# Half the tokens of six blocks through seven half-width products, with their activation sums on GpSimd

## The chip, the cores and the metric

The kernel runs on one core of one Trainium2 chip. The metric is the time of one execution on the device in microseconds; for the kernel before it is the median of three runs. The profile shows one execution, engine by engine: PE is TensorE, DVE VectorE, ACT ScalarE, POOL GpSimd and SP SyncE, which here only issues DMAs.

## The reference

An attention with a relative-position bias feeds a two-layer network with a snake-like activation (8 batches, 8 heads, 576 positions, head dimension 64; 512 wide, 2048 hidden):

```python
scores = scale * np.matmul(q, k.transpose(0, 1, 3, 2))
scores = scores + bias.transpose(2, 0, 1)[None, :, :, :]
attn = np.exp(scores - np.max(scores, axis=-1, keepdims=True))
attn = attn / (np.sum(attn, axis=-1, keepdims=True) + 1e-09)
x = np.matmul(attn, v).transpose(0, 2, 1, 3).reshape(4608, 512)
h = x @ w_in
s = np.sin(alpha * h)
g = h + s * s / (alpha + 1e-09)
out = g @ w_out
```

The 8 x 576 positions are the 4608 tokens (rows) of the second part.

## The kernel before

The tokens go through the second part in nine blocks of 512, numbered 0 to 8; the attentions go by batch, 0 to 7. The loop over `t` plans attention `t`, then the first layer and the activation of block `t` (`plan_moe_in`), then block `t`'s output matmuls (`plan_mo`), which run as filling during attention `t` + 1. Blocks 7 and 8 have no attention behind them; their output matmuls are the tail.

In an attention PE computes scores of two heads (`qT`, `kT`) into a pair of PSUM banks, ACT takes the exponential of a unit of 128x1024 into `u`, DVE multiplies the part near the diagonal by the exponential of the bias (`m2r`, `mhr`; lines 740 and 726: two SBUF inputs, written in place), and PE multiplies the result by `v`. DVE normalizes (lines 954 and 955) and SP's transposing DMAs, or PE, write the result into `xT`. Several units make a run: the first has three units of head pair 0 (key columns 0 to 2), the next a unit of the last 64 keys, the next the fourth column of pair 0 and two columns of pair 1. The product with `v` for pair 0 needs the bias multiplications of all four columns.

In the snake stage PE makes `h` for 16 slices of 128 hidden units, ACT takes the sine (line 1070), ACT or DVE squares it (lines 1077 and 1079), and DVE forms `g` (line 1084). A row is 128 tokens of a block; its output is 16 matmuls of 512 columns into one PSUM bank, which ACT or DVE copies to `outs` (lines 539 and 541) and SP stores.

The tail already uses Strassen's form in Winograd's variant (`plan_half`): for two rows together, the activations and `w_out` are split into 2 x 2 quarters, and seven products of 8 matmuls of 256 columns take the place of eight such products. It needs four sums of activation quarters (`pre`, 128x1024 elements) and four differences of weight quarters (`wsum`, made once by `plan_wsum` in attentions 2 to 5, one in each, in four pieces). The products are combined when they are taken from PSUM.

The order of every engine is fixed when the kernel is built. `Plan` holds tasks with dependencies, a priority and a planned duration for each engine that may do them, and picks the next by planned start and priority. Tasks with `fill` set are let into the attentions by a quota, or where PE would otherwise stand for longer than `FILL_GAP`. On the chip each engine keeps this order and waits on semaphores. PSUM banks are given out by tag (`BANKS`): `mo` and `av` share banks 6 and 7, scores and `h` use 0 to 5.

POOL issues the DMAs that convert types. When the first slice of `g` of block `b` is done, it loads `v` of batch `b` + 1 (`load_v16`) and stages `k` and `q` of batch `b` + 2 in DRAM as f16 (`stage_kq`). SP later transposes these into `kT` and `qT` (`load_kqT`), and POOL copies the last 64 keys of `kT` into `kt` (`load_kt`).

Of the kernel before, what the change touches and what calls it, by code (L numbers as in the profile page):

```python
# [10 lines left out]
F16 = mybir.dt.float16  # L11
# [29 lines left out]
class Task:  # L41
    def __init__(self, engs, emit, deps, pri, nb=0.0):
        self.engs, self.emit, self.deps, self.pri, self.nb = engs, emit, list(deps), pri, nb
        self.allocs = []
        self.marks = []
        self.offs = None
        self.s_only = self.fill = False
        self.pad = ()
        self.end = self.eng = None

# [11 lines left out]
class Plan:  # L62
# [86 lines left out]
    def run(self, t0):  # L149
        free = {e: t0 for e in ("PE", "ACT", "DVE", "POOL", "SP")}  # L150
        todo = list(self.tasks)
        while todo:
# [4 lines left out]
            for t in todo:  # L157
# [6 lines left out]
                for e in t.engs:  # L164
# [106 lines left out]
def kernel(  # L271
# [75 lines left out]

    xT = sgl.tile([128, NP, XN], F16, name="xT")
    wsum = sgl.tile([128, 4, NF // 2, DM // 2], F16, name="wsum")


    natx = tp.tile([128, NF * DM], F16, name="natx", tag="g", bufs=2)
# [24 lines left out]

    def new_sq():
        return tp.tile([128, DM], F16, name="sq", tag="sq", bufs=NBUF["sq"])

    def new_outs():
        return tp.tile([128, DM], F32, name="outs", tag="outs", bufs=NBUF["outs"])
# [3 lines left out]
    def bank(b, n=1):  # L386
        k = b.banks[0]
        return pb[:, k, :] if n == 1 else pb[:, k : k + n, :]

    def stage_kq(t):  # L390
        for dst, src in ((staged_k, k), (staged_q, q)):
            nc.gpsimd.dma_start(
                out=dst.ap()[t].rearrange("s (h d) -> s h d", h=H),
                in_=src[t].rearrange("h s d -> s h d"),
            )
# [138 lines left out]
    def k_of(e):  # L534
        return {"ACT": nc.scalar, "DVE": nc.vector, "POOL": nc.gpsimd}[e]
# [510 lines left out]
    def plan_moe_in(b, tbl):  # L1046
# [5 lines left out]
        for f in range(NF):  # L1052
# [28 lines left out]
            def gg(e, f=f, h=h, sq=sq):  # L1081
                if f == 0:
                    gcell[b].v = new_g()
                nc.vector.scalar_tensor_tensor(  # L1084
                    out=gcell[b].v[:, f, :], in0=sq.v, scalar=inv_a[:, f : f + 1], in1=h.v,
                    op0=ALU.mult, op1=ALU.add,
                )
# [10 lines left out]
            for n in steps:  # L1098
# [16 lines left out]
    mo_last = []  # L1115

    def plan_mo(b, a):

# [52 lines left out]
    def plan_half(b, a):  # L1171
# [21 lines left out]
        def pre(k, x, y, op, deps):  # L1193

            def sm(e):
                if k == 0:
                    u.v = new_u()
                nc.vector.tensor_tensor(out=sums(k), in0=x(), in1=y(), op=op)
# [69 lines left out]
        for (c0, c1), k in zip(cuts, "ef"):  # L1268
            p = prod(k, lambda: act(1, 1), ws(3), True, [], c0, c1)
            add(k, 2, (o2[0], 1, 0), [p, z], o2[1], False, c0, c1)  # L1270

    def set_table(name):
        nc.scalar.preload_act_table_set(name)  # L1273
        plan.sin = name == SIN_SET
# [8 lines left out]
    for t in range(T):  # L1283
# [29 lines left out]

        tbl = [plan.add({"ACT": D_TBL}, swap, exps, PB)]
        if 1 <= t < T - 1:
            plan.add({"SP": 5.5}, turn_in, [], PB + 9000, after=tbl + [
                x for tt, _, _, x in xdone if tt == t and "SP" in x.engs])
        if t == T - 1:
            tail_alone(t, PB + 10015)
        sins = []  # L1320
# [42 lines left out]
```

## Time and profile before

| what | value |
|---|---|
| median of 3 runs | 369.78 us (369.11 to 369.91) |
| the profiled execution | 369.14 us |
| its span, first to last instruction | 367.2 us |
| granted TensorE clock, mean over the span | 1.000 |
| time of one block in the middle (block 2's snake stage and attention 3) | 39.55 us |
| DMA, mean over the span | 110 GB/s |

How to read it: "busy" is the union of an engine's instructions. A row of the timeline gives the start (us from the span's start), the duration from the first to the last of a group, the engine, the source line, the operation, the tiles written and read, the shape and the count, and in brackets the idle time ahead of it with what ended it. Most matmuls are recorded on one helper line (459), so they are told apart by tiles: `xT,w_in` is the first layer, `w_out,g` the output, `wsum` a Strassen product, `qT,kT` the scores, `v,u` and `vh,u` the products with `v`. Matmuls overlap in time: the pace of a row of them is shorter than the duration of one.

### The profile page before, as it was taken

The page shows a single profiled execution, that of the slowest core. Times are in us where ns is not written, and L with a number is a line of the kernel's source. Part 1 is how long each engine was busy: PE and PEld are TensorE (multiplying, and loading weights), DVE is VectorE, ACT ScalarE, POOL GpSimd, SP SyncE. Part 2 cuts the span into 40 slices and gives each one's busy share as a digit, 9 for nine tenths or more (in the row PEclk, how much of TensorE's full clock was granted, in tenths as well). Part 3 has the DMA queues.
Part 4 walks back from the last instruction along what each step waited for, and adds up shares of the span by engine and source line. Part 5 has one row for each costly group of instructions (what it writes and reads, how often), then busy time and mean ns, then how long its engine had stood idle before and what let it go on. Part 6 is the DMA issues. An engine that isn't in the chain of part 4 may idle for free.

```text
span 367.2 us, 9181 instructions
## 1 busy us (share of the span) xinstructions
PE 359.4 (98%) x3664; PEld 204.4 (56%) x3664; DVE 279.2 (76%) x609; ACT 316.5 (86%) x437; POOL 91.7 (25%) x133
## 2 busy tenths in 40 slices
PE   7989999999999999999999999999999999999996
PEld 3564545644464455784554456445566455445885
DVE  4797957678777967697759777796769675999972
ACT  3998999899997999799989999799979997999411
POOL 8487350063000910064003700090006000000000
PEclk9999999999999999999999999999999999999999
DMA  9999999689624993199918992699339321000222
GB/s 169 204 160 203 198 165 155 145 71 131 120 59 96 107 167 91 51 160 143 131 48 145 125 166 61 109 98 181 77 68 159 71 59 49 8 1 31 71 75 86
DMA packets 150266, 40.49 MB, mean 110 GB/s; under 512 B 137208, under 2 KB 145616, under 8 KB 150224
## 3 DMA queue, kind: packets, MB, share of 16 engines
q0 software_dynamic: 96032, 17.67, 59.6%
q1 hardware_dynamic: 54016, 22.16, 25.2%
q8 instruction: 28, 0.46, 0.6%
q14 instruction: 14, 0.11, 0.1%
q10 hardware_dynamic: 176, 0.09, 0.1%
HBM read 37.73 MB, written 16.56 MB: 148 GB/s over the span
## 4 chain that ended last, share of the span: by engine, by line
PE 90%; ACT 6%; DVE 2%; issue 1%; ACTq 0%
PE pb L459 89%; ACT u L709 3%; ACT s L1070 1%; DVE u L740 1%; ACT sq L1077 1%; PE pb L1026 1%; PE pb L558 0%; ACT kT L539 0%; ACT qT L539 0%; PE pb L552 0%; DVE qT L541 0%; DVE xn L955 0%; DVE outs L1246 0%; DVE zz L510 0%; DVE u L726 0%
## 5 line engine op out<-in xcount | busy, mean ns | idle before, releaser
L709 ACT ACTIVATE u<-pb 128x1024 f16<-128x1024 f32 (+1 forms) x146 | 137.3, 1016 | 7.9 <-PE pb L459 6.4
L459 PE MATMUL pb<-xT,w_in 128*128 128x512 f16 (+4 forms) x704 | 127.6, 340 | 0.0
L459 PE MATMUL pb<-w_out,g 128*128 128x512 f16 (+1 forms) x512 | 119.0, 366 | 0.0
L1084 DVE SCALAR_TENSOR_TENSOR g<-sq,inv_a,pb 128x512 f16<-128x512 f16 x144 | 101.1, 742 | 4.5 <-ACT sq L1077 2.6
L1070 ACT ACTIVATE s<-pb,alphaT 128x512 f16<-128x512 f32 x144 | 93.0, 693 | 11.4 <-PE pb L459 10.4
L459 PEld LDWEIGHTS <-w_in 128*128 128x128 f16 x704 | 64.7, 98 | 57.2 <-issue 0.3
L740 DVE TENSOR_TENSOR u<-u,m2r 128x512 f16<-128x512 f16 (+1 forms) x128 | 62.0, 491 | 30.4 <-ACT u L709 27.9
L459 PEld LDWEIGHTS <-g 128*128 128x128 f16 x552 | 50.1, 98 | 47.4 <-issue 6.2
L459 PEld LDWEIGHTS <-u 128*128 128x128 f16 x1280 | 56.2, 97 | 11.3 <-issue 3.6
L404 POOL COPY kt<-kT 64x256 f16<-64x256 f16 x12 | 4.8, 396 | 171.4 <-DMA kT<-staged_k 171.2
L1077 ACT ACTIVATE sq<-s 128x512 f16<-128x512 f16 x73 | 45.5, 637 | 0.9
L459 PE MATMUL pb<-v,u 128*128 128x65 f16 x1024 | 44.0, 193 | 0.2 <-DVE u L740 0.2
L459 PE MATMUL pb<-qT,kT 64*128 64x64 f16 (+1 forms) x512 | 41.9, 285 | 1.7 <-ACT u L709 0.8
L1079 DVE TENSOR_TENSOR sq<-s 128x512 f16<-128x512 f16 x71 | 29.3, 421 | 12.5 <-ACT s L1070 11.5
L955 DVE TENSOR_TENSOR xn<-pb,rd 128x256 f16<-128x256 f32 (+2 forms) x59 | 28.5, 483 | 2.0
L459 PEld LDWEIGHTS <-kT 64*128 64x128 f16 x512 | 16.3, 94 | 22.9 <-issue 16.1
L459 PE MATMUL pb<-vh,u 128*128 128x130 f16 x128 | 28.2, 220 | 0.0
L409 POOL DMA_DIRECT2D v<-in_v_dram x28 | 24.8, 895 | 4.1 <-DMA nat<-in_k_dram 2.2
L954 DVE RECIPROCAL rd<-pb 128x4 f32<-128x4 f32 (+2 forms) x59 | 10.9, 185 | 13.2 <-PE pb L459 13.2
L541 DVE COPY outs<-pb 128x512 f32<-128x512 f32 x26 | 17.8, 685 | 3.0 <-PE pb L459 3.0
L1273 ACT ACT_TABLE_LOAD x15 | 19.2, 1283 | 0.3
L539 ACT ACTIVATE u<-pb 128x256 f32<-128x256 f32 x12 | 4.6, 384 | 15.8 <-PE pb L459 15.8
(86 smaller groups left out, 233.4 us busy)
## 6 DMA issues: line engine op xcount, KB each, us to landing
out_dram<-outs SPq DMA_DIRECT2D x28, 256.0 KB, 4.0
v<-in_v_dram POOLq DMA_DIRECT2D x28, 128.0 KB, 4.7
staged_k<-in_k_dram POOLq DMA_DIRECT2D x6, 576.0 KB, 9.2
staged_q<-in_q_dram POOLq DMA_DIRECT2D x6, 576.0 KB, 12.6
w_in<-in_moe_w_in_dram POOLq DMA_DIRECT2D x4, 512.0 KB, 8.9
w_out<-in_moe_w_out_dram POOLq DMA_DIRECT2D x4, 512.0 KB, 14.8
out_dram<-outs SPq DMA_DIRECT2D x15, 128.0 KB, 1.7
w_out<-in_v_dram SPq DMA_DIRECT2D x6, 128.0 KB, 5.9
```

Source lines behind the costliest of these rows:

```text
L409: nc.gpsimd.dma_start(out=vs[t % 2][:, c, :, 0:D], in_=vp[128 * c : 128 * c + 128],)
L459: nc.tensor.matmul(out=out, lhsT=lhsT, rhs=rhs, start=start, stop=stop, skip_group_check=go_on)
L541: k_of(e).tensor_copy(out=o, in_=i)
L709: nc.scalar.activation(out=o, in_=x, func=AF.Exp, scale=0.125)
L740: nc.vector.tensor_tensor(out=io, in0=io, in1=m2[:, 2 * p : 2 * p + 2, x0 : x0 + hi - lo], op=ALU.mult)
L954: nc.vector.reciprocal(out=r, in_=x[:, :, :, D])
L955: nc.vector.tensor_tensor(out=xn[:, 0:n].rearrange("p c (z d) -> p c z d", z=2), in0=x[:, :, :, 0:D], in1=r.unsqueeze(3).to_broadcast([128 ...
L1070: nc.scalar.activation(out=s16.v, in_=h.v, func=AF.Sin, scale=alphaT[:, f : f + 1])
L1077: nc.scalar.activation(out=sq.v, in_=s16.v, func=AF.Square)
L1079: k_of(e).tensor_tensor(out=sq.v, in0=s16.v, in1=s16.v, op=ALU.mult)
L1084: nc.vector.scalar_tensor_tensor(out=gcell[b].v[:, f, :], in0=sq.v, scalar=inv_a[:, f : f + 1], in1=h.v, op0=ALU.mult, op1=ALU.add,)
L1273: nc.scalar.preload_act_table_set(name)
```

## The change

In blocks 1 to 6, rows 0 and 1 keep their 16 matmuls; rows 2 and 3 go through a new function, `plan_chain`. It makes four activation sums per block, all on GpSimd, and seven products of 8 matmuls of 256 columns, two products to a PSUM bank. Each product is taken from PSUM by a copy or an add of 256 columns, into `outs` or, for one of them, into the tile `zz`. The sums start when the last slice of the block's `g` is done, which is when the next attention begins; the second needs the first, the fourth needs the second, and the third is written in place into `g`. A 256-wide filling matmul counts half of the quota.

Around it: all sixteen pieces of the weight differences are made in attention 1 (four in each of attentions 2 to 5 before). The load of `v` becomes a task of its own on POOL, behind the copies of `kt`; the staging of `k` and `q` is put behind the fourth sum. In the tail, the third and fourth activation sums of block 7's two pairs of rows go to GpSimd; those of block 8 stay on DVE. In the built order ACT also has one square less in most of the snake stages, and DVE one more.

```diff
-NBUF = {"ut": 2, "u": 2, "g": 2, "s16": 3, "sq": 3, "outs": 5, "xn": 6}
+NBUF = {"ut": 2, "ss": 1, "u": 2, "g": 2, "s16": 3, "sq": 3, "outs": 5, "xn": 6}
...
-            if over and min((x[0] for x in cands["PE"]), default=1e9) > free["PE"] + FILL_GAP:
+            if over and min((x[0] for x in cands["PE"]), default=1e9) > free["PE"] + FILL_GAP * min(
+                    x[1].part for x in over):
...
-                self.used += 1
+                self.used += t.part
...
+T_SUM = 3.6
+MIX = "nnssss"
+CH = ("mo", "mo", "mo", "st")
+ON = ("POOL", "POOL")
...
-                if f == 0 and 1 <= b < T - 1:
-                    nc.gpsimd.tensor_copy(out=tick, in_=gcell[b].v[0:1, 0, 0:1])
-                    load_v16(b + 1)
-                    if b + 2 < T:
-                        stage_kq(b + 2)
...
+            if f == 0 and 1 <= b < T - 1:
+
+                def issue(e):
+                    nc.gpsimd.tensor_copy(out=tick, in_=gcell[b].v[0:1, 0, 0:1])
+                    load_v16(b + 1)
+
+                x = plan.add({"POOL": 6.0}, issue, [gdone[(b, 0)]] + kq_in[-1:], PB + 9500, use=[gbuf[b]])
+                staged.append(x)
+                if b + 2 < T:
+                    to_stage.append((b + 2, x))
...
-                nc.vector.tensor_tensor(out=sums(k), in0=x(), in1=y(), op=op)
-
-            return plan.add({"DVE": 0.63}, sm, deps, base - 100, new=[ub] if k == 0 else [],
+                k_of(e).tensor_tensor(out=sums(k), in0=x(), in1=y(), op=op)
+
+            on = {"POOL": T_SUM} if b < T and k > 1 else {"DVE": 0.63}
+            return plan.add(on, sm, deps, PB + 10900 if b < T else base - 100, new=[ub] if k == 0 else [],
...
+    def plan_chain(b, a):
...
+        gall = [gdone[(b, f)] for f in range(NF)]
...
+        def pre(on, out, x, y, op, deps, first=False):
+
+            def sm(e):
+                if first:
+                    sv.v = new_ss()
+                k_of(e).tensor_tensor(out=out(), in0=x(), in1=y(), op=op)
+
+            return plan.add({on: T_SUM if on == "POOL" else 0.63}, sm, deps, base - 100, new=[sb] if first else [],
+                            use=[gbuf[b]] if first else [sb, gbuf[b]])
...
+        s1 = pre(ON[0], lambda: sums(0), lambda: act(1, 0), lambda: act(1, 1), ALU.add, gall, True)
+        s2 = pre(ON[1], lambda: sums(1), lambda: sums(0), lambda: act(0, 0), ALU.subtract, [s1])
+        s3 = pre("POOL", lambda: act(1, 0), lambda: act(0, 0), lambda: act(1, 0), ALU.subtract, [s1])
+        s4 = pre("POOL", lambda: sums(2), lambda: act(0, 1), lambda: sums(1), ALU.subtract, [s2])
+        p = prod(0, lambda: act(0, 0), wq(0, 0), gall)
+        x = take(0, (2, 0), None, [p])
+        p = prod(1, lambda: act(0, 1), wq(1, 0), [])
+        c11 = take(1, (0, 0), (2, 0), [p, x], True)
+        yield
+        p = prod(2, lambda: sums(1), ws(1), [s2, x] + wdone)
+        y = take(2, (1, 1), (2, 0), [p, x], True)
+        p = prod(3, lambda: act(1, 0), ws(2), [s3])
+        v = take(3, (1, 0), (1, 1), [p, y])
+        yield
+        p = prod(4, lambda: sums(0), ws(0), [])
+        w = take(4, (0, 1), (1, 1), [p, y])
+        c22 = take(4, (1, 1), (1, 0), [p, v, w])
+        p = prod(5, lambda: act(1, 1), ws(3), [])
+        take(5, (1, 0), (1, 0), [p, v, c22], last=True)
+        yield
+        p = prod(6, lambda: sums(2), wq(1, 1), [s4])
+        take(6, (0, 1), (0, 1), [p, w, c11], last=True)
+        if to_stage:
+            t, x = to_stage.pop()
+            plan.add({"POOL": 4.5}, lambda e: stage_kq(t), [x, s4], base)
+        yield
...
-            if 2 <= t < 6:
-                plan_wsum(t - 2, exps[3:15:3])
+            if t == 1:
+                for i in range(4):
+                    plan_wsum(i, exps[3 * i + 1 : 3 * i + 4] + exps[3 * i + 3 : 3 * i + 4])
...
-            for a in range(4):
-                plan_mo(t, a)
+            if t:
+                rows, ch = iter((0, 1)), plan_chain(t, 2)
+                for x in MIX:
+                    if x == "n":
+                        plan_mo(t, next(rows))
+                    else:
+                        next(ch)
+            else:
+                for a in range(4):
+                    plan_mo(t, a)
```

`prod` plans the 8 matmuls of a product in the half bank `at(k)`, as filling with `part` = 1/2; `take` copies (ACT or DVE) or adds (DVE) that half bank into `put(i, j)` and, at a row's last quarter, has SP store the row.

More of the change, by code (lines that the diff above doesn't have):

```diff
@@ L1270, in plan_half, with act, sums, at @@
             add(k, 2, (o2[0], 1, 0), [p, z], o2[1], False, c0, c1)
+    def plan_chain(b, a):
+        H2, n = NF // 2, DM // 2
+        sv, sb = Cell(), Buf("ss")
+        bk = [Buf(x) for x in CH]
+        bv = [Cell() for _ in range(4)]
+        o = Cell(), Cell()
+        ob = Buf("outs"), Buf("outs")
+        gall = [gdone[(b, f)] for f in range(NF)]
+        base = 500000000 + 4 * b + a
+        def act(i, j):
+            return gcell[b].v[:, H2 * j : H2 * j + H2, 128 * (a + i) : 128 * (a + i) + 128]
+        def pre(on, out, x, y, op, deps, first=False):
[5 more added lines that the diff above has]
+                            use=[gbuf[b]] if first else [sb, gbuf[b]])
+        def sums(k):
+            return sv.v[:, 2 * k : 2 * k + 2].rearrange("p k (f t) -> p (k f) t", f=H2 // 2)
+        def at(k):
+            return bv[k // 2].v[:, n * (k % 2) : n * (k % 2) + n]
+        def put(i, j):
+            if i == 2:
+                return xv.bitcast(F32)
+            return o[i].v[:, n * j : n * j + n]
+        def prod(k, x, w, deps):
+            for f in range(H2):
+                new = f == 0 and k % 2 == 0
+                def mm(e, f=f, new=new):
+                    if new:
+                        bv[k // 2].v = bank(bk[k // 2])
+                    full(at(k), x()[:, f], w()[:, f], f == 0, f == H2 - 1)
+                mo_last[:] = [plan.add({"PE": t_pe(n)}, mm, mo_last[:] + deps, base,
+                                       new=[bk[k // 2]] if new else [],
+                                       use=([] if new else [bk[k // 2]]) + [sb, gbuf[b]])]
+                mo_last[0].fill = True
+                mo_last[0].part = n / DM
+            return mo_last[0]
+        def wq(i, j):
+            return lambda: w_out16[:, H2 * i : H2 * i + H2, n * j : n * j + n]
+        def ws(k):
+            return lambda: wsum[:, k]
+        def store(i):
+            r = 512 * b + 128 * (a + i)
+            nc.sync.dma_start(out=out[r : r + 128, :], in_=o[i].v)
+        def take(k, to, x, deps, new=False, last=False):
+            i, j = to
+            def ev(e):
+                if new:
+                    o[i].v = new_outs()
+                if x is None:
+                    copy_on(e, put(i, j), at(k))
+                else:
+                    nc.vector.tensor_tensor(out=put(i, j), in0=at(k), in1=put(*x), op=ALU.add)
+                if last:
+                    store(i)
+            bs = [sb] if i == 2 else [] if new else [ob[i]]
+            return plan.add({"DVE": t_dve(n)} if x else {"ACT": t_act(n), "DVE": t_dve(n)}, ev, deps, CP_PRI,
+                            new=[ob[i]] if new else [], use=[bk[k // 2]] + bs)
+        s1 = pre(ON[0], lambda: sums(0), lambda: act(1, 0), lambda: act(1, 1), ALU.add, gall, True)
[24 more added lines that the diff above has]
+        yield
@@ L1315 @@
         if 1 <= t < T - 1:
[L1316 to L1317 removed]
+            kq_in.append(plan.add({"SP": 5.5}, turn_in, [], PB + 9000, after=tbl + [
+                x for tt, _, _, x in xdone if tt == t and "SP" in x.engs]))
         if t == T - 1:
```

7 lines of the change are left out of this document (6 added, 1 removed).

## The prediction

> **What bounds the kernel now.** I read the page's totals first, then the chain that ended last, then the busy times of single blocks (from the start of one block's snake stage to the next), and last the instructions of one attention in order of time.
>
> ```profile
> span 367.2 us, 9181 instructions
> PE 359.4 (98%) x3664; PEld 204.4 (56%) x3664; DVE 279.2 (76%) x609; ACT 316.5 (86%) x437; POOL 91.7 (25%) x133
> ...
> PE 90%; ACT 6%; DVE 2%; issue 1%; ACTq 0%
> ```
> ```profile
> 111.10:150.65 39.55, 39.55 (x389) 20.35 (x386) 31.02 (x68) 36.09 (x47) 10.29 (x11) 1.00 1.00 115
> ...
> 309.17:367.20 58.03, 54.52 (x418) 35.95 (x415) 45.72 (x87) 35.09 (x64) 0.00 (x0) 1.00 0.14 44
> ```
>
> In the second fence the columns are the stretch, its length, then PE, weight loads, DVE, ACT and POOL busy with their counts, the granted clock and DMA. PE is busy for 39.55 of a block's 39.55 us at clock 1.00, and 90% of the chain is PE. So matmul columns saved are time saved, and any instruction that PE, whose order is fixed, has to wait for is time lost. ACT has 3.5 us free in the block and DVE 8.5; POOL seems to have plenty.
>
> **The matmuls removed.** Two of a block's four 128-token rows took 2 x 16 matmuls of 512 columns; now they take 7 products of 8 matmuls of 256 columns.
>
> ```profile
> 129.96 0.39 PE L459 MATMUL pb<-w_out,g 128*128 128x512 f16 x1
> ...
> 136.25 2.33 PE L459 MATMUL pb<-w_out,g 128*128 128x512 f16 x10
> ```
> ```profile
> 346.91 2.78 PE L459 MATMUL pb<-wsum,u 128*128 128x256 f16 x24
> ```
> ```profile
> L459 PE MATMUL pb<-wsum,u 128*128 128x256 f16 x96 | 11.2, 273 | 0.0
> ```
>
> One lasts 0.39 and ten last 2.33, so the pace is (2.33 - 0.39) / 9 = 0.2156 us. For 256 columns it is (2.78 - 0.273) / 23 = 0.109. A block pays 32 x 0.2156 = 6.90 before and 56 x 0.109 = 6.10 after: 0.80 us saved, 4.8 in six blocks, if nothing makes PE wait.
>
> **The evictions, on DVE.** Two copies of 512 columns go, one copy of 256 and seven adds of 256 come.
>
> ```profile
> L1079 DVE TENSOR_TENSOR sq<-s 128x512 f16<-128x512 f16 x71 | 29.3, 421 | 12.5 <-ACT s L1070 11.5
> ...
> L541 DVE COPY outs<-pb 128x512 f32<-128x512 f32 x26 | 17.8, 685 | 3.0 <-PE pb L459 3.0
> ...
> L1246 DVE TENSOR_TENSOR outs<-pb,u 128x256 f32<-128x256 f32 x15 | 6.3, 423 | 4.2 <-PE pb L459 2.3 <-ACT u L539 1.8
> ...
> L1198 DVE TENSOR_TENSOR u<-g 128x1024 f16<-128x1024 f16 x8 | 5.4, 684 | 0.0
> ...
> L1165 DVE TENSOR_TENSOR wsum<-w_out 128x512 f16<-128x512 f16 x8 | 3.3, 417 | 0.0
> ```
>
> That is 8 x 0.423 - 2 x 0.685 = 2.0 us more a block, and one square of 0.42 moves from ACT to DVE; blocks 2 to 5 lose four weight differences of 0.417 each. DVE's 8.5 free us hide it: cost nothing. With that cover gone it would be up to 2.4 us a block.
>
> **The weight differences, all in attention 1 now.** Sixteen of 0.417 us make 6.7.
>
> ```profile
> 49.00:73.00 24.00, 24.00 (x317) 13.57 (x316) 15.83 (x43) 22.35 (x27) 2.79 (x3) 1.00 1.48 148
> ```
>
> DVE has 24.00 - 15.83 = 8.2 us free there, so they fit, but tightly. Bounds: nothing, and all 6.7 if each stands just ahead of a multiplication that PE awaits. I take 0.3, since four of them in attention 3 left PE without a gap (first fences).
>
> **The activation sums, on POOL.** This decides. Each block gets four sums of 128x1024 f16 on GpSimd (684 ns each on DVE, above), the second behind the first, the fourth behind the second, from the last g of the block on. They sit in the attention's first half, where DVE multiplies the exponentials with the bias, with two SBUF inputs each time. POOL has no sum of that size in the trace; the nearest rows are its 128x128 multiplications in block 0.
>
> ```profile
> 16.50 0.76 POOL L726 TENSOR_TENSOR u<-u,mhr 128x128 f16<-128x128 f16 x1
> ...
> 22.21 0.44 POOL L726 TENSOR_TENSOR u<-u,mhr 128x128 f16<-128x128 f16 x1
> ```
> ```profile
> L740 DVE TENSOR_TENSOR u<-u,m2r x2: 546/664/782, 16.4 to 16.9; 128x768 f16<-128x768 f16 x2
> ```
> ```profile
> 22.18 0.42 DVE L955 TENSOR_TENSOR xn<-pb,rd 128x256 f16<-128x256 f32 x1
> ...
> 23.39 0.69 DVE L740 TENSOR_TENSOR u<-u,m2r 128x768 f16<-128x768 f16 x1
> ```
>
> At 22.21 POOL runs beside a DVE instruction that reads PSUM and one SBUF tile: 0.44 for POOL, 0.42 for DVE, nobody is disturbed. At 16.50 it meets two bias multiplications. The first, already under way, takes its usual 546 ns, and POOL needs 0.76 instead of 0.44: it stood still. The second then takes 782: it stood still for 236 ns. Neither is stretched, they take turns by whole instructions. So 128 elements hold the port for 0.236 us, and 1024 would hold it for 8 x 0.236 = 1.9 us.
>
> [...]
>
> Now the first half of an attention, that of block 3's attention as it is:
>
> ```profile
> 127.15 2.80 POOL L392 DMA_DIRECT2D staged_q<-in_q_dram  x1
> 127.30 1.40 DVE L1084 SCALAR_TENSOR_TENSOR g<-sq,inv_a,pb 128x512 f16<-128x512 f16 x2
> ...
> 128.47 0.82 PE L459 MATMUL pb<-qT,kT 64*128 64x512 f16 x6
> 128.92 3.77 ACT L709 ACTIVATE u<-pb 128x1024 f16<-128x1024 f32 x4
> ...
> 129.98 0.42 DVE L740 TENSOR_TENSOR u<-u,m2r 128x512 f16<-128x512 f16 x1 [1.28 <-ACT u L709]
> ...
> 130.90 0.56 DVE L740 TENSOR_TENSOR u<-u,m2r 128x768 f16<-128x768 f16 x1
> ...
> 131.81 0.56 DVE L740 TENSOR_TENSOR u<-u,m2r 128x768 f16<-128x768 f16 x1 [0.36 <-ACT u L709]
> ...
> 132.89 0.28 DVE L726 TENSOR_TENSOR u<-u,mhr 128x256 f16<-128x256 f16 x1
> ...
> 133.93 0.42 DVE L740 TENSOR_TENSOR u<-u,m2r 128x512 f16<-128x512 f16 x1 [0.43 <-ACT u L709]
> ...
> 134.50 0.22 PE L459 MATMUL pb<-vh,u 128*128 128x130 f16 x1
> ```
>
> The last g ends at 127.30 + 1.40 = 128.70, so the first sum holds the port from about 128.9 (0.2 of its 0.44 is not the hold). DVE's first bias multiplication comes at 129.98 and waits. From there they alternate: sum, multiplication, sum, multiplication, sum, multiplication, sum, then the last two (the small one of the third column too). PE's first attention-times-v at 134.50 needs all four wide ones. They are done at 128.9 + 4 x 1.9 + (0.42 + 0.56 + 0.56 + 0.28 + 0.42 = 2.24) = 138.7, and PE follows 0.15 later as it does now (134.50 less 133.93 + 0.42), at 138.9. In the changed order one more output matmul stands ahead of that instruction, so PE reaches it at 134.50 + 0.22 = 134.72. It waits 4.2 us, in each of six attentions. Behind it queue the scores of pair 1's last columns and so ACT's eighth exponential: nothing catches up, as PE had no free time. If POOL wins every turn, the four holds run on end and the multiplications follow: the same end within 0.2 us.
>
> Bounds: below, no hold beyond the 128 elements shown, a wait of 0; above, 8 x 0.44 = 3.5 us a sum, a wait of 10.6. I take 1.9, as the 236 ns is a hold and the 0.44 a whole instruction with its start.
>
> **The staging of k and q** moves behind the sums on POOL's queue.
>
> ```profile
> 125.45 2.28 POOL L392 DMA_DIRECT2D staged_k<-in_k_dram  x1
> ```
> ```profile
> staged_k<-in_k_dram POOLq DMA_DIRECT2D x6, 576.0 KB, 9.2
> staged_q<-in_q_dram POOLq DMA_DIRECT2D x6, 576.0 KB, 12.6
> ```
> ```profile
> 154.49 2.37 SPq L398 DMA_TRANSPOSE kT<-staged_k  x1
> 156.97 2.27 SPq L399 DMA_TRANSPOSE qT<-staged_q  x1
> ```
>
> It goes from 125.45 to about 138.9 for k, and q follows 1.7 later (127.15 above). From issue to landing they take 9.2 and 12.6 us: 138.9 + 9.2 = 148.1 for k and 140.6 + 12.6 = 153.2 for q, ahead of SP's transposes at 154.49 and 156.97 (and those move back with PE's wait). Cost nothing; a late q would next hold the scores of the following attention. The loads of v keep their place, as only their wait on the copies ahead of them is now written out.
>
> **The tail.** In block 7's two pairs the third and fourth sums go to POOL too.
>
> ```profile
> 320.00:344.00 24.00, 24.00 (x135) 12.99 (x134) 23.72 (x43) 22.84 (x41) 0.00 (x0) 1.00 0.05 18
> ```
>
> DVE is full there. It loses 4 x 0.684 = 2.7 us of sums and gains two waits of 1.9 for the second sums that stand behind POOL's: 1.1 more. Bounds 0 (PE has other products) and 1.1; I take 0.6.
>
> **The sum.** The profiled execution took 369.14 (span 367.2 and 1.9 around it): 369.14 + 6 x (4.2 - 0.8) + 0.3 + 0.6 = 390.4. The median of the runs, 369.78, lies 0.6 above that execution, so I forecast 391.0.
>
> **The rivals,** each moved up by the same 0.6:
>
> Long instructions let DVE in between. For it: only 128 and 256 elements are shown. Against it: the two rows that stood still. Then nothing waits and 4.8 is gained, less 0.3: 365.2. This is the other side: it decides wherever a hold is under about 0.85 us, as then the last multiplication still meets its date (128.9 + 4 x 0.85 + 2.24 = 134.5).
>
> The port is split evenly. Each multiplication takes twice as long, and with the copy of a row (0.69) between them they end near 135.1 instead of 134.4: a wait of 0.5. 6 x (0.5 - 0.8) + 0.9 = -0.9: 368.9. Against it: the first multiplication's unchanged 546.
>
> A sum takes 3.5 us throughout: 6 x (10.6 - 0.8) + 0.9 = 59.7, so 429.5. Against it: three quarters of POOL's 0.44 would have to be work, where 0.236 was seen.
>
> PE's clock falls during the wait.
>
> ```profile
> 360.00:368.00 8.00, 3.69 (x42) 3.22 (x39) 1.86 (x5) 0.77 (x2) 0.00 (x0) 0.96 0.21 66
> ```
>
> The granted clock is 1.00 everywhere but here, where PE has finished. If after each wait PE ran at half clock for as long as it had stood, each would cost 4.2 / 2 = 2.1 more: 403.6. [...] No row before the end shows such a gap.
>
> **How the numbers follow.** My forecast with the clock held has 0.52; its own range, holds from 1.6 to 2.4 us, is 384 to 403 (6 x 4 x 0.5 = 12 above, 6 x 4 x 0.3 = 7 below). The fallen clock has 0.12, DVE let in 0.25, the split port 0.06, the long sum 0.05. The range has to reach the third: 364.5 to 406. About 0.2% is what a measurement of this kernel tells from no change, 0.7 us. Faster: 0.25 and about half of the split port, 0.28; within: 0.03; slower: 0.69.
>
> **What would show it.** Right: in every attention from the second on, one idle stretch of PE near 4 us ahead of its first attention-times-v, put down to DVE's multiplications; bias multiplications of over 2 us there and of 0.42 to 0.56 later; GpSimd sums of 2 to 3 us; blocks of about 43 us, with output matmuls at 0.109 as before. Wrong: PE still full and blocks of 38.8 us; then the hold does not grow with the instruction. A clock below 1.00 behind the gaps gives the dearer case; a wait for qT or kT the staging.

## The result, and the profile after

The changed kernel takes 401.16 us (median of 4 runs, 398.17 to 402.78), the kernel before 369.68 on the same chip: 1.085 times as long, 95% interval 1.078 to 1.091. The forecast was 391.0 with a range of 364.5 to 406. Two of the runs below (the weight differences early, and the short exponentials with late evictions) were profiled in an execution of over 600 us at a clock near 0.56, so only their times are used. The profiled execution of the changed kernel is the one of 398.17. The page's totals and the end of its chain of waits:

```profile
span 396.4 us, 9541 instructions
...
PE 367.9 (93%) x3808; PEld 220.6 (56%) x3808; DVE 321.3 (81%) x647; ACT 312.9 (79%) x431; POOL 155.1 (39%) x161
...
PE 62%; DVE 18%; ACT 7%; DMA 6%; issue 3%; POOL 1%; SPq 0%; DVEq 0%
```

PE's share of the chain fell from 90% to 62%, DVE's rose from 2% to 18%: PE now waits for DVE (15.0 us in twelve waits for multiplications of L750, one of 0.2 before). The stretches, with the columns of the prediction's second fence: attention 1, attention 2, a middle block (all from the third attention to the sixth take 44.3), and the tail.

```profile
25.86:70.73 44.87, 44.02 (x552) 24.24 (x549) 37.80 (x92) 42.65 (x60) 17.14 (x28) 1.00 1.40 167
70.73:115.78 45.05, 41.54 (x432) 23.66 (x428) 36.92 (x75) 37.01 (x51) 19.41 (x15) 1.00 0.87 89
...
248.65:292.96 44.31, 41.23 (x410) 23.09 (x407) 36.43 (x71) 35.96 (x47) 19.42 (x15) 0.96 0.94 103
...
338.20:392.84 54.64, 52.90 (x366) 34.74 (x362) 45.63 (x81) 33.92 (x62) 8.86 (x4) 1.00 0.13 40
```

```profile
26.19:69.93 43.74, 43.20 (x549) 23.79 (x546) 33.05 (x75) 41.73 (x60) 16.93 (x28) 1.00 1.39 169
69.93:111.75 41.82, 41.72 (x409) 21.63 (x406) 31.20 (x72) 38.20 (x53) 10.39 (x11) 1.00 0.91 103
309.82:363.69 53.87, 53.87 (x400) 35.42 (x398) 45.41 (x86) 34.60 (x63) 0.00 (x0) 1.00 0.13 40
```

The second fence has the same stretches of the kernel before. Attention 1 is 1.1 us longer, attention 2 3.2, a middle block 4.8 (44.31 less 39.55), the tail 0.8. In the middle block DVE shows 7 us more busy time (36.43, 29.40 in the stretch 230.56 to 270.11 of before) with only some 2.4 us more work by the prediction's count, and the granted clock is 0.96. The timeline of one attention shows both; it begins at 220.85 where the prediction's began at 128.47:

```profile
220.85 0.82 PE L469 MATMUL pb<-qT,kT 64*128 64x512 f16 x6
221.25 2.12 POOL L1307 TENSOR_TENSOR ss<-g 128x1024 f16<-128x1024 f16 x1 [2.13 <-PE pb L469]
...
222.36 1.28 DVE L750 TENSOR_TENSOR u<-u,m2r 128x512 f16<-128x512 f16 x1 [1.29 <-ACT u L719]
...
223.44 2.19 POOL L1307 TENSOR_TENSOR ss<-ss,g 128x1024 f16<-128x1024 f16 x1
...
224.11 1.93 DVE L750 TENSOR_TENSOR u<-u,m2r 128x768 f16<-128x768 f16 x1
224.25 1.24 PE L469 MATMUL pb<-w_out,g 128*128 128x512 f16 x5 [0.43 <-DVE xn L965]
...
225.59 2.43 POOL L1307 TENSOR_TENSOR g<-g 128x1024 f16<-128x1024 f16 x1
...
225.97 0.68 DVE L551 COPY outs<-pb 128x512 f32<-128x512 f32 x1
...
226.57 1.87 DVE L750 TENSOR_TENSOR u<-u,m2r 128x768 f16<-128x768 f16 x1
227.48 0.22 PE L469 MATMUL pb<-vh,u 128*128 128x130 f16 x1
...
227.99 2.43 POOL L1307 TENSOR_TENSOR ss<-g,ss 128x1024 f16<-128x1024 f16 x1
228.36 2.20 DVE L736 TENSOR_TENSOR u<-u,mhr 128x256 f16<-128x256 f16 x1
228.49 0.35 PE L469 MATMUL pb<-v,u 128*128 128x65 f16 x6 [0.44 <-DVE u L750]
...
230.49 0.75 DVE L750 TENSOR_TENSOR u<-u,m2r 128x512 f16<-128x512 f16 x2
230.95 0.33 PE L469 MATMUL pb<-v,u 128*128 128x65 f16 x5 [1.96 <-DVE u L750]
...
232.61 3.23 PE L469 MATMUL pb<-w_out,g 128*128 128x512 f16 x14
```

Read POOL and DVE against each other. A DVE multiplication starts at 222.36, in the middle of the first sum, and ends at 223.64, when that sum has been over for 0.27 us: of its 1.28 us, 0.42 is work. The second sum then runs until 225.63, and the multiplication beside it ends at 226.04. Four sums and four waiting multiplications alternate until 230.5. DVE's copy of an output row at 225.97, which reads PSUM, runs beside the third sum in its usual 0.68. PE idles three times (0.43, 0.44, 1.96). Behind that, fourteen output matmuls take 3.23 us. The row carries the shape of its first one; by form five of them have 512 columns and nine 256, and the five last 616 ns each, where the same matmuls lasted 380 before (the prediction's 0.39):

```profile
L469 PE MATMUL pb<-w_out,g 128*128 128x512 f16 x5 | 2.2, 616 | 0.0
```

Over that stretch the clock reads

```profile
231.20:234.70 3.50, 3.50 (x15) 1.03 (x13) 1.81 (x5) 2.84 (x3) 3.50 (x2) 0.51 0.49 33
```

0.51: PE runs at half clock. Five of the six attentions have such a stretch of 3.41 us; they begin 44.4 us apart (142.5, 186.9, 231.2, 275.6, 320.0), which is 13 times 3.41, while the blocks come every 44.3.

### The profile page after: what moved, and what is told of

It reads as the page before. It is cut to its first block, busy times and chain, and to the rows that moved or that the text cites. A ratio compares the mean times of both kernels' runs of the same rounds, so it can differ in the third digit from the quotient of the medians.

```text
span 396.4 us, 9541 instructions
## 1 busy us (share of the span) xinstructions
PE 367.9 (93%) x3808; PEld 220.6 (56%) x3808; DVE 321.3 (81%) x647; ACT 312.9 (79%) x431; POOL 155.1 (39%) x161
## 4 chain that ended last, share of the span: by engine, by line
PE 62%; DVE 18%; ACT 7%; DMA 6%; issue 3%; POOL 1%; SPq 0%; DVEq 0%
PE pb L469 61%; DVE u L750 8%; ACT u L719 6%; DMA w_out<-in_moe_w_out_dram 5%; DVE u L736 3%; DVE g L1094 2%; DVE outs L1361 1%; DMA m2r<-e_dram 1%; DVE sq L1089 1%; DVE u L1213 1%; DVE outs L551 1%; DMA e_dram<-e_sb 1%; ACT s L1080 1%; DVE xn L965 1%; PE pb L1036 0%
## 5 line engine op out<-in xcount | busy, mean ns | idle before, releaser
L750 DVE TENSOR_TENSOR u<-u,m2r 128x512 f16<-128x512 f16 (+1 forms) x128 | 81.8, 651 | 17.1 <-ACT u L719 15.9
L469 PE MATMUL pb<-w_out,g 128*128 128x512 f16 (+1 forms) x416 | 87.2, 352 | 2.7 <-DVE xn L965 1.9
L469 PEld LDWEIGHTS <-g 128*128 128x128 f16 x552 | 52.5, 100 | 46.3 <-issue 18.6
L469 PE MATMUL pb<-v,u 128*128 128x65 f16 x1024 | 46.0, 194 | 15.0 <-DVE u L750 15.0
L469 PE MATMUL pb<-qT,kT 64*128 64x64 f16 (+1 forms) x512 | 45.7, 299 | 2.4 <-ACT u L719 1.1
L1087 ACT ACTIVATE sq<-s 128x512 f16<-128x512 f16 x69 | 44.0, 641 | 2.1 <-DVE g L1094 1.2
L1089 DVE TENSOR_TENSOR sq<-s 128x512 f16<-128x512 f16 x75 | 32.2, 435 | 10.9 <-ACT s L1080 10.1
L1307 POOL TENSOR_TENSOR ss<-g 128x1024 f16<-128x1024 f16 x6 | 12.7, 2117 | 24.0 <-DVE g L1094 15.3
L469 PE MATMUL pb<-wsum,g 128*128 128x256 f16 (+1 forms) x136 | 18.6, 266 | 0.9
```

Of the source, the lines that this page charges most:

```text
L469: nc.tensor.matmul(out=out, lhsT=lhsT, rhs=rhs, start=start, stop=stop, skip_group_check=go_on)
L750: nc.vector.tensor_tensor(out=io, in0=io, in1=m2[:, 2 * p : 2 * p + 2, x0 : x0 + hi - lo], op=ALU.mult)
L1087: nc.scalar.activation(out=sq.v, in_=s16.v, func=AF.Square)
L1089: k_of(e).tensor_tensor(out=sq.v, in0=s16.v, in1=s16.v, op=ALU.mult)
L1307: k_of(e).tensor_tensor(out=out(), in0=x(), in1=y(), op=op)
```

## The experiments

Each run is compared with runs of the kernel before on the same chip; its median was 369.89 us beside the first four runs, 369.53 beside the next three, 369.37 beside the two with short exponentials and 369.95 beside the last three.

**The sums alone.** The kernel before with the four sums on GpSimd added to each of blocks 1 to 6; no product reads them, and the third goes into the tile `ss`, not in place into `g`.

```diff
+    def plan_sums(b, a):
...
+                nc.gpsimd.tensor_tensor(out=out(), in0=x(), in1=y(), op=op)
...
+        s1 = pre(lambda: sums(0), lambda: act(1, 0), lambda: act(1, 1), ALU.add, gall, True)
```

> The kernel before, with the same four GpSimd sums per block 1 to 6 added behind the staging of k and q, their results used by nobody; PE's order is that of the kernel before. Port theory: the price of the sums alone, PE waits of about 3 us ahead of the first attention-times-v (the first sum starts some 1.3 us later than in the changed kernel, behind the staging's issue) and the half clock in most blocks: 369.7 + 6 x (3 to 5.5) = 388 to 402. Rivals: the sums are idle work of an idle engine, 369.7 within 1.

Measured: 405.38 us (403.57 to 406.74), ratio 1.095 (1.090 to 1.100), above the 388 to 402 expected. A middle block:

```profile
257.77:301.88 44.11, 40.04 (x384) 20.27 (x383) 35.84 (x64) 36.59 (x48) 19.36 (x15) 1.00 0.92 103
```

PE has the matmuls of before in the order of before, and 4.1 us (44.11 less 40.04) of idle time in the block even where the clock stays at 1.00; over the whole execution the granted clock was 0.975, so it fell in other places. The sums by themselves do all the harm and more; the products, the evictions and the weight differences aren't needed for it.

**The sums on DVE.** The changed kernel with its chain's four sums moved.

```diff
-ON = ("POOL", "POOL")
+ON = ("DVE", "DVE")
...
-        s3 = pre("POOL", lambda: act(1, 0), lambda: act(0, 0), lambda: act(1, 0), ALU.subtract, [s1])
-        s4 = pre("POOL", lambda: sums(2), lambda: act(0, 1), lambda: sums(1), ALU.subtract, [s2])
+        s3 = pre("DVE", lambda: act(1, 0), lambda: act(0, 0), lambda: act(1, 0), ALU.subtract, [s1])
+        s4 = pre("DVE", lambda: sums(2), lambda: act(0, 1), lambda: sums(1), ALU.subtract, [s2])
```

> The four activation sums of blocks 1 to 6 on VectorE instead of GpSimd (0.68 us each there), planned at 0.63; the tail's two sums a pair stay on GpSimd. Port theory (DVE's bias multiplications stood behind GpSimd's sums): no bias multiplication over 0.8 us in the attentions, no gap of PE above 0.5 us, clock 1.00; 401.2 less 6 x (about 3.3 of waits + 1.5 of half clock + 0.5 of small gaps) = 369.5, at best 366 if DVE's extra 2.7 us a block are hidden. Rival (the chain's own evictions or the matmuls of 256 columns cost the time): still 395 or more. Rival (weight differences and staging moved): little change, 398 to 402.

Measured: 374.27 us (373.38 to 374.39), ratio 1.011 (1.007 to 1.015). The middle blocks are back near where they were (39.56 to 40.02; 39.55 to 39.71 before), though DVE has 2.7 us of sums more (four of 0.69). The shortest of them:

```profile
232.72:272.28 39.56, 39.31 (x411) 22.99 (x409) 33.38 (x74) 36.48 (x48) 10.43 (x11) 1.00 1.06 117
```

So 27 of the 31 us go with the engine of the sums. Of the 4.4 us that are left over, 2.6 lie in the tail (56.48; here the order differs and PE waits twice 1.4 us for `g`).

**Zeros for the sums.** POOL writes the four tiles, in the same places of the same order, and reads nothing. Products 3, 4, 5 and 7 of each chain multiply zeros (the sixth takes a quarter of `g` as it is).

```diff
-                k_of(e).tensor_tensor(out=out(), in0=x(), in1=y(), op=op)
+                nc.gpsimd.memset(out(), 0.0)
```

> The order of all engines stays that of the changed kernel, but in the place of the four sums of a block GpSimd fills the same tiles with zeros, an instruction that writes SBUF and reads none: the products 3 to 7 are of zeros. Port theory as I stated it (two readers of SBUF take turns): multiplications of 0.42 to 0.56 us again, PE without the gaps, 6 x 0.8 us less than before plus what the tail and attention 1 cost (about 0.8 and 1.1): 366 to 368. If any GpSimd instruction blocked DVE: waits in proportion to the fill's length, 375 or more. Rivals (evictions, moved staging, moved weight differences): 395 or more, as all of these are kept.

Measured: 371.27 us (370.33 to 373.83), ratio 1.003 (1.000 to 1.006). The zeros, the multiplications, and a block:

```profile
L1307 POOL MEMSET ss<- x18: 945/1006/1007, 84.3 to 288.8; 128x1024 f16 x18
```
```profile
L750 DVE TENSOR_TENSOR u<-u,m2r x128: 410/546/780, 15.7 to 308.1; 128x512 f16<-128x512 f16 x64, 128x768 f16<-128x768 f16 x64
```
```profile
194.15:233.49 39.34, 39.09 (x410) 22.84 (x408) 31.38 (x71) 35.96 (x47) 13.98 (x15) 1.00 1.04 116
```

The changed kernel's multiplications, for comparison:

```profile
L750 DVE TENSOR_TENSOR u<-u,m2r x128: 408/546/2477, 14.4 to 333.4; 128x512 f16<-128x512 f16 x64, 128x768 f16<-128x768 f16 x64
```

With zeros the longest multiplication is 780 ns (782 in the kernel before, both in the first 27 us) instead of 2477. This run alone doesn't show that writing holds nobody, though: zeros needn't wait for the last `g`, so the fills come earlier (the first at 84.3, the changed kernel's first sum at 89.8) and need not meet a multiplication at all. The short-exponential runs further down fill the gap. In the kernel before with short exponentials two fills of 128x1024 last from 168.26 to 171.23, and two multiplications beside them keep their 0.42 and 0.55:

```profile
168.26 2.97 POOL L845 MEMSET u<- 128x1024 f16 x2
```
```profile
169.71 0.42 DVE L742 TENSOR_TENSOR u<-u,m2r 128x512 f16<-128x512 f16 x1 [1.30 <-ACT u L711]
...
170.60 0.55 DVE L742 TENSOR_TENSOR u<-u,m2r 128x768 f16<-128x768 f16 x1
```

So the fills, which read nothing, held no multiplication there, and the sums, which read, held one for up to 2.5 us. But the block is only 0.21 us shorter than before, not 0.80 (0 to 0.22 in the other middle blocks): a second thing is missing, taken up below. The time, too, is above the 366 to 368 expected.

**The sums in eighths.** The same sums, each as eight instructions of 128 elements.

```diff
-                k_of(e).tensor_tensor(out=out(), in0=x(), in1=y(), op=op)
+                o, i0, i1 = out(), x(), y()
+                for f in range(H2):
+                    k_of(e).tensor_tensor(out=o[:, f], in0=i0[:, f], in1=i1[:, f], op=op)
```

> Each sum as eight GpSimd instructions of 128 elements, everything else in the changed kernel's order. Port theory with a hold of one instruction: a hold is 0.25 us, DVE gets in between, multiplications of up to about 0.85 us; the multiplications keep pace with the exponentials (1.03 us each) and the waits nearly vanish: 366 to 373. If the hold belonged to the work and not to the instruction (bandwidth shared, or GpSimd always first): still 390 or more.

Measured: 372.93 us (371.15 to 376.62), ratio 1.0085 (1.005 to 1.012). 

```profile
L750 DVE TENSOR_TENSOR u<-u,m2r x128: 405/548/824, 17.1 to 310.0; 128x512 f16<-128x512 f16 x64, 128x768 f16<-128x768 f16 x64
```
```profile
235.34:274.68 39.34, 39.16 (x410) 22.87 (x407) 32.41 (x71) 36.03 (x47) 26.36 (x43) 1.00 1.02 114
```

The same elements read by the same engine, and no multiplication over 824 ns, where the whole sums made one of 2477: what held the multiplications was one instruction, not the four sums' work as a whole. In the changed kernel, beside whole sums of 2.11 to 2.44 us, multiplications lasted up to 2.48, beside pieces of 0.48 to 0.57 (means) up to 0.82, and beside the two fills, 2.97 us together, their 0.42 and 0.55.

**Work in the wait.** Eleven matmuls without use where PE idles, so that only the clock can change.

```diff
+                if k == 0 and t > 1 and p0 == 0 and nq == 3:
+                    for _ in range(11):
+                        full(av.v[:, 0:512], id_sb, w_in16[:, 0, 0:512], True, True)
```

> Eleven matmuls of 512 columns (11 x 0.2156 = 2.4 us) without use stand ahead of the first attention-times-v of each attention from the second on, where PE idles 0.4 and 2.0 us. They fill the idle time and nothing else is to move: DVE's last bias multiplication ends when it did, and PE's next step after it waits for that. Theory (about 1.7 us of each block's loss is PE at half clock behind the idle time): granted clock 1.00 everywhere, no run of fourteen output matmuls at 0.23 that takes 3.2 us, blocks of 42.6 instead of 44.3, so some 387 to 393 in all. Rival (the clock falls for another reason, such as POOL's or DVE's work, or the half clock costs nothing since PE waits anyway): blocks of 44.3 or more, 398 to 405.

Measured: 393.78 us (393.27 to 394.24), ratio 1.066 (1.063 to 1.068).

```profile
247.28:289.96 42.68, 41.80 (x421) 23.89 (x419) 36.46 (x71) 35.97 (x47) 19.37 (x15) 1.00 1.00 107
```
```profile
232.23 2.23 PE L469 MATMUL pb<-w_out,g 128*128 128x512 f16 x14
```
```profile
L469 PE MATMUL pb<-w_out,g 128*128 128x512 f16 x5 | 1.3, 381 | 0.0
```

Sixty-six matmuls more make the kernel 7.4 us faster. In the middle block the clock is 1.00, and so it is from 231.50 to 234.50, where the fourteen output matmuls run; over the span the profiled execution shows 0.981, the other three 1.000. The fourteen take 2.23 instead of 3.23, the five of 512 columns 381 ns each instead of 616, a block 1.63 us less. The scatter goes too (1 us between the runs, 4.6 in the changed kernel).

**The tail's sums back on DVE** (`plan.add({"DVE": 0.63}, ...)` for all of them, as before the change).

> The changed kernel with the third and fourth sums of block 7's two pairs on DVE again. Theory (the two second sums that stand behind POOL's sums cost PE a gap): the stretch from the last snake stage to the end takes 53.9 as before instead of 54.6, with no PE gap of 1.6 us for a g of DVE; blocks unchanged at 44.3. Rival (DVE is full there and its 2.7 us of sums back cost as much): 54.6 or more.

Measured: one execution, 400.85 us. The tail and attention 2:

```profile
70.99:118.69 47.70, 44.18 (x432) 24.59 (x429) 37.00 (x75) 36.99 (x51) 19.39 (x15) 0.93 0.78 84
...
341.31:395.51 54.20, 52.67 (x368) 34.67 (x362) 46.23 (x88) 32.77 (x60) 0.00 (x0) 1.00 0.13 41
```

Neither side: 54.20 lies between 54.64 and the 53.87 of before; the gap for `g` is gone and one of 1.5 us for a sum of DVE is there. The other row shows one way in which executions of this design differ: here the clock also fell in attention 2 (0.93, against 1.00 in the profile after), and that stretch took 2.65 us more.

**The weight differences early,** in the kernel before.

```diff
-            if 2 <= t < 6:
-                plan_wsum(t - 2, exps[3:15:3])
+            if t == 1:
+                for i in range(4):
+                    plan_wsum(i, exps[3 * i + 1 : 3 * i + 4] + exps[3 * i + 3 : 3 * i + 4])
```

> The kernel before with its sixteen weight differences in attention 1 instead of attentions 2 to 5. Theory (they stand ahead of bias multiplications that PE awaits; the changed kernel's stretch of attention 1 is 1.1 us longer than before): attention 1's stretch grows by about 1.1 and the later ones shrink by 0 to 0.1, 370.2 to 370.8 in all. Rival, my prediction's own 0.3: 369.7 to 370.2. If it is below 369.7 the 1.1 comes from something else in that stretch.

Measured: 369.74 us, ratio 1.0006 (0.997 to 1.004). The interval, -1.0 to 1.4 us, tells nothing, 0.3 and 1.1 apart only weakly; the median, 0.2 above the kernel before, is nearer to the first two. The rows of attention 1 have another reading of its 1.1 us. In that stretch PE's output matmuls are, after and before:

```profile
L469 PE MATMUL pb<-w_out,g 128*128 128x512 f16 x57 | 14.1, 379 | 0.3 <-DMA w_out<-in_moe_w_out_dram 0.3
```
```profile
L459 PE MATMUL pb<-w_out,g 128*128 128x512 f16 x54 | 13.3, 380 | 0.0
```

Three more are done there (3 x 0.2156 = 0.65, no loss, as attention 2 has them less), and one comes before its `w_out` has landed, a gap of 0.3. That reading rests on the rows; no run took it apart.

**Why the columns saved don't show.** The zeros kernel and the kernel before, both with ACT relieved: the wide exponentials leave out 128 of 1024 columns, and GpSimd writes zeros there.

```diff
+                if t > 1:
+                    o, x = o[:, :, 0:448], x[:, :, 0:448]
...
+                    if t > 1:
+                        nc.gpsimd.memset(u.v[:, :, 0:8, 448:512], 0.0)
```

> The kernel with zeros for sums, whose blocks take 39.34 to 39.5 instead of the 38.75 that 0.80 us less of matmul columns would give, with ACT relieved: the sixteen wide exponentials of each attention from the second on leave out 128 of their 1024 columns (GpSimd writes zeros there at the attention's start). ACT saves some 16 x 0.107 = 1.7 us a block. Theory (the saving of matmul columns is not had since ACT, whose exponentials run end to end through the attention, sets its length): blocks fall to 38.7 to 39.0, 367.5 to 369.0 in all. Rival (PE pays for the shorter products itself, by more switches between operands): blocks stay at 39.3 to 39.5, 370.5 to 371.5.

> The kernel before with the same shortened exponentials. Theory (PE is the bound there, ACT only just below it): blocks fall by 0.2 at most, 368.5 to 369.7 in all. If they fall by 0.4 or more, ACT bounds the kernel before as well, and a saving of columns could not show in either.

Measured: 368.99 us, ratio 0.998 (0.995 to 1.000), and 369.53 us, ratio 1.001 (0.999 to 1.004). A block of each:

```profile
229.79:268.80 39.01, 38.87 (x410) 22.64 (x408) 31.25 (x71) 34.35 (x47) 15.59 (x17) 1.00 1.07 117
```
```profile
230.50:269.99 39.49, 39.49 (x384) 20.08 (x383) 29.28 (x64) 34.87 (x48) 12.00 (x13) 1.00 1.01 115
```

The same 1.6 to 1.7 us off ACT gives 0.33 with fewer columns on PE (39.34 to 39.01) and 0.06 without (39.55 to 39.49). So with fewer columns ACT's exponentials, which run nearly end to end through the attention, hold PE back, but that is half of the missing 0.59 (0.80 less 0.21). Another pause of PE is seen in the timeline of the zeros kernel with short exponentials:

```profile
265.07 0.27 PE L469 MATMUL pb<-wsum,g 128*128 128x256 f16 x1
...
265.38 0.42 DVE L1365 TENSOR_TENSOR outs<-pb,outs 128x256 f32<-128x256 f32 x1 [0.34 <-PE pb L469]
...
265.85 0.41 PE L469 MATMUL pb<-v,u 128*128 128x65 f16 x8
265.92 0.42 DVE L1365 TENSOR_TENSOR outs<-pb,outs 128x256 f32<-128x256 f32 x1
...
266.40 0.92 PE L469 MATMUL pb<-wsum,g 128*128 128x256 f16 x7
```

Eight matmuls of 65 columns from 265.85 would be through at about 266.1 (an estimate: eight take 0.41 and one 0.19, so the next comes 0.03 later); the sixth product's other seven start at 266.40, just behind DVE's second eviction of the fifth product (265.92 + 0.42 = 266.34). The two products share a PSUM bank, and in the built program the sixth waits there for a semaphore of DVE, by the author's reading of it. The next run moves these two evictions behind the sixth product:

```diff
         p = prod(4, lambda: sums(0), ws(0), [])
+        p = prod(5, lambda: act(1, 1), ws(3), [])
         w = take(4, (0, 1), (1, 1), [p, y])
         c22 = take(4, (1, 1), (1, 0), [p, v, w])
-        p = prod(5, lambda: act(1, 1), ws(3), [])
```

> The kernel with zeros for sums and short exponentials, where a block takes 39.0, with one change of order: the two evictions of the fifth product stand behind the sixth product, its neighbour in the PSUM bank, instead of ahead of it. In that kernel PE's remaining matmuls of the sixth product wait for a semaphore of DVE and start 0.06 us after those evictions end, 0.31 late. Theory (the rest of the missing saving, 0.25 us a block, is this wait between the two products that share a bank): no such pause, blocks of 38.7 to 38.8 (39.55 - 0.80 = 38.75), 367.0 to 367.7 in all. Rival (the wait only moves to the next product or to the bank's next user): blocks stay at 39.0, 369.0.

Measured: 368.06 us, ratio 0.995 (0.993 to 0.998). By the ratios 0.8 us less than without the move, where 1.3 to 2.0 were expected; the intervals overlap, so this run alone leaves the size open. The same move in the whole computation, with the sums in eighths:

> The changed kernel with its sums in eighths and the same late evictions: the whole computation. Theory (0.31 us a block is this wait; ACT keeps the rest): blocks of 39.1 to 39.3 instead of 39.34 to 39.56, 371.0 to 372.0 in all against 372.9. Rival (ACT's chain sets the block alone): 372.5 to 373.5.

Measured: 370.59 us, ratio 1.0025 (0.9997 to 1.0054), against 1.0085 without the move; the two intervals just overlap. In its timeline the sixth product's seven matmuls follow without a pause (from 320.22), but of its blocks from the third attention on only one took the 39.1 to 39.3 us expected (39.22; three others took 39.69, 39.84 and 40.63, the last two with PE waiting 0.66 and 1.44 for a transposing DMA of `xT`). So what the move is worth isn't settled. It is the best form of the change that was tried, and it doesn't beat the kernel before. Two of its thirteen runs took over 382 us. The profiled execution is one of these, and shows what happened:

```profile
251.20 10.13 DVE L750 TENSOR_TENSOR u<-u,m2r 128x512 f16<-128x512 f16 x1 [1.29 <-ACT u L719]
...
251.81 3.11 POOL L1309 TENSOR_TENSOR ss<-ss,g 128x128 f16<-128x128 f16 x8
...
...
257.95 3.10 POOL L1309 TENSOR_TENSOR ss<-g,ss 128x128 f16<-128x128 f16 x8
...
261.94 2.29 PE L469 MATMUL pb<-w_out,g 128*128 128x512 f16 x5 [9.29 <-DVE xn L965]
```

One multiplication stood until the last of POOL's short sums was through. POOL's eight pieces took 3.10 us there, 3.7 to 4.3 in the eighths kernel, where the two engines took turns.

**Less on ACT.** The same with the tail's sums on DVE and the squares of each block's last four columns of `h` always on DVE.

```diff
-            y = plan.add(SQ, sqr, [x], pri - 5,
+            y = plan.add({"DVE": 0.38} if 1 <= b < T - 1 and f >= 12 else SQ, sqr, [x], pri - 5,
```

> The same, with the tail's sums back on DVE and the squares of a block's last four columns of h always on DVE (two squares of 0.62 us less on ACT in each of blocks 1 to 6). Theory (ACT holds back 0.3 us a block): blocks of 38.8 to 39.1, 369 to 371 in all, about the kernel before. Rival (DVE, with 0.84 us more ahead of the last g, makes the sums and so PE's first product late): blocks of 39.3 or more, 371.5 to 374.

Measured: 375.51 us, ratio 1.016 (1.013 to 1.019), blocks of 40.2 to 40.7: the rival's side, and more than its 374. The scores begin 17.4 to 18.1 us into a block, 16.5 to 16.7 in four of the five blocks of the eighths kernel, which fits the rival. PE also waits for DVE's copies of output rows, 2.5 us in all, six times. How much of the 4.9 us over the run before each of the two costs, no run took apart; whether less work on ACT alone would pay stays open.

## Why the prediction was right, and where it wasn't

The cause, its place and its form were right: POOL's sums and DVE's multiplications alternate by whole instructions. "Port" is the prediction's word for what they take turns at; the runs show the turns, not what is shared. The prediction had the last multiplication done at 138.7 on a clock where the scores begin at 128.47; here they begin at 220.85, so it would be 231.1, and the one that PE waited for, the first of the two in the row of 230.49, ended at 230.49 + 0.41 = 230.90. A sum lasts 2.11 to 2.44 us, not 1.9; but from the first sum's start to that multiplication's end it is 9.65 us, where 9.84 were worked out, and less the 2.24 of multiplications that leaves 1.85 us for each of four holds, an estimate by which the rest of a sum's time is no hold. The four runs on the sums bear it out: sums alone do it, sums on DVE, fills that don't read and sums in short pieces don't. That also drops the three rivals on the port: DVE let in between, an even split, 3.5 us a sum.

**PE's wait** was sized at 4.2 us and shows 0.43 + 0.44 + 1.96 = 2.83. The failing step: "needs all four wide ones". Only the later matmuls of that product do; PE ran some 1.1 us of it in between (227.48 to 228.06 and 228.49 to 229.00), and so idled in pieces, not in one stretch near 4 us. The queue for `xn`, 0.43, was not named at all.

**The clock** is where the choice was wrong. The forecast held it at 1.00 (0.52) and gave its fall 0.12, for 403.6; it fell in five of six attentions. No row of before shows PE at half clock beside a wait, and no run shows it for as long as PE had stood, so the 4.2 / 2 of that rival and the choice against it were both the author's estimate. The runs showed 0.51 in stretches of 3.41 us, though PE was not idle throughout ahead of one: from 227.83 to 231.24 it worked 1.02 us, and its longest idle stretch was 1.96. Cut along the grid of 3.41 us, the trace tells more:

```profile
98.12:101.54 3.42, 2.07 (x18) 1.09 (x19) 3.17 (x7) 1.38 (x2) 3.42 (x3) 1.00 0.00 0
...
227.83:231.24 3.41, 1.02 (x24) 0.73 (x22) 3.40 (x4) 0.88 (x1) 3.41 (x3) 1.00 0.24 77
```

In attention 2 (first row) the same waits fall into two windows with 2.13 and 2.07 us of PE each, and the clock held; ahead of each of the five half-clock stretches PE was busy for 0.64 to 1.02. From 2.6 us to the end of PE's work no other window of that grid has less than 1.96 us of PE (357.50 to 360.91, in the tail), and none is followed by half clock. So in this execution the clock fell where the waits came together in one window and held where they fell into two. That this also makes the scatter of the executions is the author's guess; no run took it apart. The fall cost 1.63 us in a block by the run with work in the wait, not 2.1.

**The saving** was 0.80 us a block, "if nothing makes PE wait". Without the port's waits 0.21 is left. ACT takes 0.33: the block was held to be bound by PE, with 3.5 us free on ACT, but ACT's free time lies elsewhere: in the kernel before (230.56 to 270.11) its longest idle stretches are 1.06 us at the start of the snake stage and 0.4 at the block's end, and within the attention none is over 0.2. **The evictions** were costed at nothing since DVE has room; a price not in DVE's time but in the order shows, as the second product in a bank waits for the eviction of the first. The pause of 0.3 is seen, and gone in the timeline of the whole computation with late evictions; what it is worth in time was not settled.

If these simply add, a middle block comes to -0.80 + 2.83 + 1.63 + 0.59 = 4.25 of the measured 4.76 us; the other 0.5 was not traced. For the profiled execution the sum of the prediction was 390.4, and 398.17 came: the wait gives 6 x (2.83 - 4.2) = -8.2, the clock 5 x 1.63 = 8.2, the saving not had 6 x 0.59 = 3.5, attention 1 some 0.8, and six times the untraced 0.5, in all 7.3 of 7.8. So it is luck that the oversized wait and the missing fall of the clock cancelled, and that 401.16 lies in the forecast's own range of 384 to 403; what the total lacked is the saving that wasn't had and the untraced part.

**The tail** was put at 0.6 and took 0.77; sums back on DVE took 0.44 of it away in one execution. **The weight differences** were put at 0.3; the run that moved them alone shows 0.2, within its uncertainty nothing. **The staging** was hidden as predicted: k and q were issued at 230.4 and 232.1, and PE waits for `qT` as it did before, once in the whole execution for 0.6 us.

## What to carry to other kernels

Moving elementwise work from DVE to GpSimd can cost DVE more than it saves (401.16 us here, 374.27 with the sums on DVE). In the changed kernel the sums on GpSimd, whose operands lie in SBUF, held DVE multiplications of two SBUF operands until about their own end (1.28 to 2.20 us in the timeline, where 0.28 to 0.56 were usual), while DVE's copies from PSUM (0.68 us) went on; what has to be priced is the first deadline behind DVE, not its busy share. Where PE must wait a few us in every block, matmuls without use in the gap can pay (7.4 us here). Where PE is full and a second engine is nearly full in one stage of the block, work taken off PE in that stage may not show: of 0.80 us a block 0.21 came.

## What was not expected of the hardware

- The clock halved though no idle stretch was longer than 1.96 us (0.44 + 1.96 within one window of 3.41), and the half-clock stretches lay on a grid of 3.41 us. In the profiled execution the five windows with 0.64 to 1.02 us of PE were followed by half clock, those with 1.96 or more not.
- GpSimd instructions of 128 elements let DVE in between in the run with the sums in eighths (no multiplication over 0.824 us); with late evictions once a multiplication that takes 0.42 us lasted 10.13, with 24 of them and more beside it. It happened in 2 of 13 runs by their times, in one by the trace. What decides it stays open.
- A GpSimd sum of 128x1024 f16, beside DVE's multiplications, took 2.11 to 2.44 us, 3.1 to 3.6 times DVE's 0.684.
